# Where the sums of the first layer's weights are split, and which engine makes a low part: one change in a four-stage kernel

## Chip, core and metric

One core of a Trainium2 chip. The core has a matrix engine (TensorE, PE), VectorE (DVE), ScalarE (ACT), GpSimd (POOL) and SyncE (SP), whose queue issues nearly all DMAs. Each engine works through its own queue in order; semaphores order them against each other. The metric is the device time of one execution, in microseconds (us).

## What is computed

```python
x = attention_with_decay(q, k, v, lam)        # 2 x 768 tokens, 8 heads of 64, float32
p = domain_probs / (domain_probs.sum(-1) + 1e-9)
y = sum(p[:, e] * (relu(x @ w1[e]) @ w2[e]) for e in range(4))     # 1536 x 512, hidden 1024
h = y @ w_in                                  # hidden 2048
out = (h * sigmoid(h)) @ w_out                # 1536 x 512
```

The last two lines are the feed-forward part (FFN), which the change touches: a first layer `w_in` ("up") and a second layer `w_out` ("down").

## The kernel before

Every float32 operand of a large product is split into a high part, rounded to the matrix engine's format, and a low part, the rest; a product is the three matmul groups high x high, low x high and high x low. `split` (L144) makes the high part on ACT (L145) and the low part, a subtract, on another engine (L146), POOL unless DVE is named.

There are four stages. The first is attention, and the experts for the first 512 tokens; the second the experts for the other 1024 tokens; the third the FFN for the first 512 tokens; the fourth the FFN for the other 1024. The second and fourth use a scheme of seven products for 2 x 2 blocks, which needs sums of weight quarters. An engine's order is the order in which the program issues its instructions; nothing reorders them.

**Third stage** (the loop over `i` in `range(nb)`, 16 steps). A step does one first-layer GEMM (`gemm1`, 12 matmuls, L532, out `ph`), the sigmoid gate (`sg` on ACT, `ph` times `sg` on DVE), the split of the hidden block (`hhi` on ACT, `hlo` on DVE), and the second-layer GEMM of two steps before (`gemm2`, 12 matmuls, L589, out `po`). In steps 0 and 1 the remaining second-stage work stands in its place, and in the last two steps there is none: those GEMMs are held in `fill` for the fourth stage. Two steps, a pair, use one pair of weight blocks. `split_up` makes `ua` and `ub` (high and low) for the next pair in even steps, `split_down` `dh` and `dl` in odd ones. Beside this the stage prepares the fourth one. In even steps `left_sums` makes the four sums of the raw first-layer weights on POOL (L668) in `us`, a tile with one buffer. In odd steps `left_out` splits them (`uc` on ACT, `low` on POOL) and stores both halves to a DRAM tile `wu[i]`, and `left_kept` stores the split, unsummed blocks there. `combine` spreads eleven jobs over steps 3 to 13, which make sums (`sum`, DVE) and splits (`hi` on ACT, `lo` on DVE) of the tokens' block.

`load(0)` and `load(1)` issue the next load of raw first-layer (`u`) and second-layer (`d`) weights on SP; the buffer, one of two, must have been used up.

**Fourth stage** (the loop over `i` in `range(NV)`, 8 pairs). `pair7` issues the seven products of a pair, six matmuls each (L747, out `x`, `y`, `z`), with one or two pieces of other work from `fill` after all but the first; each is six matmuls too. `prepare` says which jobs follow which product, counted from 0. `left_in` reads the split sums of a pair and its A11 block (five slots of `ua` and `ub`), for products 1, 6, 5, 7 and 3; `left_in2` reads `uc`, for products 2 and 4. `left_in(0)` is issued in step 14 of the third stage, the others one pair ahead. `down_sums` and `down_left` make and split the sums of the second-layer weights for the second products, `down7`; `plan7` lists after which of these they are issued, and how many products or pieces later.

Of the kernel before, what the change touches and what calls it, by code (L numbers as in the profile page):

```python
# [7 lines left out]
F32 = mybir.dt.float32  # L8
F32R = mybir.dt.float32r
# [6 lines left out]
P = 128  # L16
# [10 lines left out]
HW = DM // 2  # L27
# [4 lines left out]
NV = NF  # L32


A12, A22, A21, A11 = range(4)
# [3 lines left out]
def kernel(  # L39
# [10 lines left out]
    nc = tc.nc  # L50

    def pool(stack, name, bufs=1, side="left", **kw):
        return stack.enter_context(tc.tile_pool(name=name, bufs=bufs, side=side, **kw))
# [12 lines left out]
    dram = pool(ctx, "dram", space=DRAM)  # L66

    leftp = pool(ctx, "leftp")
# [8 lines left out]

    pd = dram.tile([E, NT // GI, GI], F32, name="pd")
    wd = [dram.tile([2, P, 2 * DM], F32, name=f"wd{i}") for i in range(NV)]
    wu = [dram.tile([P, 2, 8, HW], F32, name=f"wu{i}") for i in range(NV)]  # L80

    dmask = acst.tile([P, NPAIR, 2, P], F32, name="dmask")
    qdec = acst.tile([P, NPAIR, P], F32, name="qdec")
# [30 lines left out]
    raw_t = {}  # L114
# [22 lines left out]
    def load(j, n=1):  # L137
        for _ in range(n):
            if nxt[j] < len(seq[j]):
                ph, i, src = seq[j][nxt[j]]  # L140
                nxt[j] += 1
                (load_up, load_down)[j](src, i, (ph, i))

    def split(eng, hi, lo, src):  # L144
        nc.scalar.activation(out=hi, in_=src, func=AF.Copy)  # L145
        eng.tensor_tensor(out=lo, in0=src, in1=hi.bitcast(F32), op=ALU.subtract)  # L146
# [3 lines left out]
    def up_tiles(pool_, slots=5):  # L150
        return [pool_.tile([P, slots, HW], F32R, tag=t, name=t) for t in ("ua", "ub")]

    def down_tiles(pool_):
        return [pool_.tile([P, 2, DM], F32R, tag=t, name=t) for t in ("dh", "dl")]
# [18 lines left out]
    def split_up(key, more=True):  # L173
        hi, lo = up_t[key] = up_tiles(wp)
        split(nc.gpsimd, hi[:, :4], lo[:, :4], raw_t[key, 0])
        if more:
            load(0)

    def split_down(key, eng=nc.gpsimd):
        hi, lo = down_t[key] = down_tiles(wp)  # L180
        split(eng, hi, lo, raw_t[key, 1])
        load(1)

    def up_cols(ph, f, k):
# [41 lines left out]
    def flush():  # L226
        while pending:
            pending.pop(0)()
# [9 lines left out]
    jobs = [0, 0]  # L238
# [279 lines left out]
    tmp = {}  # L518
# [137 lines left out]
    sum_t, grp_t = {}, {}  # L656

    def left_sums(key):

        u = raw_t[key, 0]  # L660
        s = leftp.tile([P, 4, HW], F32, tag="us", name="us")
        for n, (a, b, op) in enumerate([
            (u[:, A21], u[:, A22], ALU.add),
            (s[:, 0], u[:, A11], ALU.subtract),
            (u[:, A11], u[:, A21], ALU.subtract),
            (u[:, A12], s[:, 1], ALU.subtract),
        ]):
            nc.gpsimd.tensor_tensor(out=s[:, n], in0=a, in1=b, op=op)  # L668
        sum_t[key] = s
# [12 lines left out]


    def left_out(i):

        key = ("b", i)
        left_sums(key)
        src = sum_t.pop(key)

        def halves():  # L690
            load(0)
            high = leftp.tile([P, 2, 2, HW], F32R, tag="uc", name="uc").rearrange(
                "p a b n -> p (a b) n"
            )
            low = tmp["sums"].tile([P, 4, HW], F32R, tag="low", name="low")
            split(nc.gpsimd, high, low, src)
            return high, low

        def stores(tiles):
            for n, t in enumerate(tiles):  # L700
                nc.sync.dma_start(out=wu[i][:, n, 4:], in_=t.bitcast(F32))

        return halves, stores

    def left_kept(i):
        for n, t in enumerate(up_t["b", i]):
            nc.sync.dma_start(out=wu[i][:, n, :4], in_=t[:, :4].bitcast(F32))

    def left_in(i):
        grp_t[("d", i), 0] = tiles = up_tiles(wp)  # L710
        for n, t in enumerate(tiles):
            nc.sync.dma_start(out=t.bitcast(F32), in_=wu[i][:, n, A11:])

    def left_in2(i):
        t = leftp.tile([P, 2, 2, HW], F32R, tag="uc", name="uc")
# [12 lines left out]
    def unit():  # L728

        clock[0] += 1  # L730
        now = [fn for t, fn in due if t <= clock[0]]
        due[:] = [(t, fn) for t, fn in due if t > clock[0]]
        for fn in now:
            fn()

    def filler():
        if fill:
            fill.pop(0)()
        unit()
# [135 lines left out]
    def down_sums(i):  # L875

        w = raw_t[("d", i), 1].rearrange("p n (d c) -> p n d c", c=HW)
        t = tmp["d"].tile([P, 3, HW], F32, tag="ds", name="ds", bufs=2)
        for to, a, b, op in (
            (t[:, 0], w[:, 0, 1], w[:, 1, 1], ALU.add),  # L880
            (t[:, 1], t[:, 0], w[:, 0, 0], ALU.subtract),
            (t[:, 2], w[:, 1, 0], t[:, 1], ALU.subtract),
            (w[:, 0, 1], w[:, 0, 0], w[:, 0, 1], ALU.subtract),
        ):
            nc.gpsimd.tensor_tensor(out=to, in0=a, in1=b, op=op)
        d_sums[i] = {
            1: w[:, 0, 0], 2: w[:, 1, 0], 4: w[:, 1, 1],
            5: t[:, 0], 6: t[:, 1], 3: t[:, 2], 7: w[:, 0, 1],
        }

    def down_left(q):

        if q >= 7 * NV // 2:
            return
        turn = taken["dw"] % 6
        taken["dw"] += 1
        if turn < 2:
            t = tmp["d"].tile([P, 2, DM], F32R, tag="dw", name="dw", bufs=2)
        else:
            tag = ("dh", "dl")[turn % 2]  # L900
            t = wp.tile([P, 2, DM], F32R, tag=tag, name=tag)
        t = t.rearrange("p s (k c) -> p s k c", c=HW)
        for s in range(2):
            src = d_sums[q // 7 * 2 + s][ROUND[q % 7]]
            split(nc.gpsimd, t[:, s, 0], t[:, s, 1], src)
        dw_t[q] = t
# [116 lines left out]
    def plan7():  # L1023

        for g in range(NV // 2):
            q = 7 * g
            todo = [(0, 1, lambda n=q + 6: down_left(n))]
            if g + 1 < NV // 2:
                i = 2 * g + 2
                todo += [  # L1030
                    (0, 2, lambda: load(1, 2)),
                    (2, 1, lambda i=i: down_sums(i)),
                    (2, 3, lambda i=i: down_sums(i + 1)),
                ]
                for m, when, n in ((3, 1, 7), (3, 3, 8), (4, 1, 9), (4, 3, 10), (5, 2, 11), (6, 2, 12)):
                    todo.append((m, when, lambda n=q + n: down_left(n)))
            for m, when, fn in todo:
                jobs7.setdefault(q + m, []).append((when, fn))
# [118 lines left out]
    with tc.manual_schedule():  # L1157
# [62 lines left out]
        todo = {}  # L1220
# [12 lines left out]
        for i in range(NN, na):  # L1233
            gi, f = steps["a"][i]
# [89 lines left out]
        sums = ExitStack()  # L1324
        tmp["sums"] = pool(sums, "sums2", side="right")
        split_up(("b", 1), False)
        split_down(("b", 0), nc.vector)
        mixing = []
        for i in range(nb):
            flush()  # L1330
            gemm1("b", i)
            unit()
            if i < 2:
                for _ in range(KD):
                    filler()
            elif i < nb - 2:
                gemm2("b", i - 2)
            if i % 2:
                halves, stores = left
                tiles = halves()  # L1340
                for n in ([0, 1] if i == 1 else [i // 2 + 1]):
                    if n < NV:
                        left_kept(n)
                if i < nb - 1:
                    split_down(("b", (i + 1) // 2), nc.vector)
                stores(tiles)
            else:
                left = left_out(i // 2)
                if 2 <= i < nb - 2:
                    split_up(("b", i // 2 + 1), False)  # L1350
                elif i == nb - 2:
                    left_in(0)
            if i == 2:
                mixing = combine(acc_t["c", 0], acc_t["c", 1])
            elif i > 2:
                for job in mixing[i - 3:i - 2]:
                    job()
# [3 lines left out]
        tmp["d"] = pool(ctx, "dp", side="right")  # L1361
        fill += last_down("b", nb)
        plan7()
        for i in range(NV):
            jobs = {0: [lambda: left_in2(i)]}
            if i + 1 < NV:
                jobs[0].append(lambda: left_in(i + 1))
            if i == 0:
                jobs[2] = [lambda: down_sums(0)]
                jobs[4] = [lambda: down_sums(1)]  # L1370
                jobs[6] = [lambda: down_left(0), lambda: down_left(1)]
            elif i == 1:
                jobs[4] = [lambda: down_left(2), lambda: down_left(3)]
                jobs[5] = [lambda: down_left(4), lambda: down_left(5)]
            pair7(i, jobs)
        fill[-1:] = [
# [61 lines left out]
```

## Time and profile before

| | |
|---|---|
| median of 3 runs | 819.11 us (818.88 to 819.87) |
| profiled execution | 819.6 us, its span 817.8 us |
| busy: PE, DVE, ACT, POOL | 792.2, 557.3, 349.5, 504.0 us |
| PE's mean granted clock | 0.992 of full |
| third stage, from step 2 | from about 554.7 us |
| fourth stage | from about 645.6 us |

The span is what the trace covers, and the little that the execution takes beyond it lies around the program. PE's busy time is the largest of the engines'; matmuls overlap, so one that takes 389 ns follows the one before after less than that.

### The profile page before, as it was taken

To read this page: it belongs to the slowest core of one execution; us is meant where nothing else is said; L and a number is where in the kernel's file an instruction comes from. 1 tells how busy PE (TensorE), PEld (TensorE's weight loads), DVE (VectorE), ACT (ScalarE), POOL (GpSimd) and SP (SyncE) were. 2 spreads that over 40 slices of the span, in tenths; PEclk is the share of its full clock that TensorE was granted. 3 is DMA by queue.
4 is the path that set the end of the run, shared out by engine and by line. 5 is a ranking of instruction groups with operands and counts; after the bars stand their busy time and mean duration, and the time that the engine had idled before them with its cause. 6 is when DMAs were issued, how large, how long until landed. Compare 5 with 4: busy or idle time off the path is not lost.

```text
span 817.8 us, 11033 instructions
## 1 busy us (share of the span) xinstructions
PE 792.2 (97%) x4084; PEld 653.4 (80%) x4084; DVE 557.3 (68%) x785; ACT 349.5 (43%) x602; POOL 504.0 (62%) x420
## 2 busy tenths in 40 slices
PE   9999999999999999999999999999988399999997
PEld 8888888888888888888888888888766288888886
DVE  6346587786585777777777777675676256577777
ACT  4433333324454333333333333343545257745453
POOL 4846745436585666666666666657676477666753
PEclk9999999999999999999999999999999699999999
DMA  8868768453342232223222111146866726342402
GB/s 309 309 198 257 241 224 282 168 180 101 119 154 91 91 115 91 91 90 117 91 91 90 65 65 64 52 128 225 289 202 236 238 89 227 104 141 91 142 26 103
DMA packets 39479, 122.40 MB, mean 150 GB/s; under 512 B 4434, under 2 KB 4738, under 8 KB 39426
## 3 DMA queue, kind: packets, MB, share of 16 engines
q1 hardware_dynamic: 39424, 121.70, 43.9%
q8 instruction: 32, 0.52, 0.3%
q14 instruction: 21, 0.17, 0.1%
q10 hardware_dynamic: 2, 0.00, 0.0%
HBM read 93.35 MB, written 28.34 MB: 149 GB/s over the span
## 4 chain that ended last, share of the span: by engine, by line
PE 84%; DVE 4%; ACT 3%; DMA 3%; POOL 3%; issue 2%; SPq 0%; ACTq 0%; POOLq 0%; DVEq 0%
PE po L796 21%; PE ph L532 13%; PE po L589 12%; PE y L747 11%; PE z L747 8%; PE x L747 8%; PE po L976 7%; DMA wu<-low 2%; PE s L408 1%; PE xps L447 1%; DVE dl L146 1%; DMA ub<-wu 1%; POOL ub L146 1%; ACT uc L145 1%; PE xps L443 1%
## 5 line engine op out<-in xcount | busy, mean ns | idle before, releaser
L146 POOL TENSOR_TENSOR ub<-u,ua 128x1024 fp32r<-128x1024 f32 (+2 forms) x41 | 68.1, 1662 | 68.1 <-ACT ua L145 60.8
L796 PE MATMUL po<-hhi,dh 128*128 128x512 f32 x256 | 99.6, 389 | 0.0
L796 PE MATMUL po<-hhi,dl 128*128 128x512 f32 x256 | 99.6, 389 | 0.0
L796 PE MATMUL po<-hlo,dh 128*128 128x512 f32 x256 | 99.6, 389 | 0.0
L810 DVE TENSOR_TENSOR acc<-po,acc 128x512 f32<-128x512 f32 x120 | 79.4, 683 | 28.7 <-PE po L796 28.7
L146 POOL TENSOR_TENSOR dl<-d,dh 128x1024 fp32r<-128x1024 f32 (+1 forms) x33 | 77.0, 2334 | 12.3 <-ACT dh L145 12.3
L559 ACT ACTIVATE hhi<-ph 128x512 fp32r<-128x512 f32 x40 | 24.0, 599 | 126.6 <-DVE ph L553 85.3
L764 POOL TENSOR_TENSOR s<-s,s 128x512 f32<-128x512 f32 x32 | 48.6, 1520 | 31.0 <-ACT s L759 31.0
L146 POOL TENSOR_TENSOR uc<-u,uc 128x512 fp32r<-128x512 f32 x16 | 20.6, 1288 | 67.0 <-ACT uc L145 67.0
L589 PE MATMUL po<-hhi,dh 128*128 128x512 f32 (+1 forms) x208 | 57.3, 379 | 0.0
L532 PE MATMUL ph<-xhi,ub 128*128 128x512 f32 (+1 forms) x208 | 52.9, 376 | 4.5 <-POOL ub L146 4.5
L796 PEld LDWEIGHTS po<-hhi,dl 128*128 128x128 f32 x256 | 48.1, 188 | 10.1
L796 PEld LDWEIGHTS po<-hlo,dh 128*128 128x128 f32 x256 | 48.0, 188 | 9.9
L796 PEld LDWEIGHTS po<-hhi,dh 128*128 128x128 f32 x256 | 48.0, 188 | 9.9
L589 PE MATMUL po<-hhi,dl 128*128 128x512 f32 (+1 forms) x208 | 55.9, 373 | 0.0
L589 PE MATMUL po<-hlo,dh 128*128 128x512 f32 (+1 forms) x208 | 55.9, 372 | 0.0
L532 PE MATMUL ph<-xhi,ua 128*128 128x512 f32 (+1 forms) x208 | 53.8, 380 | 1.9 <-ACT ua L145 1.2
L532 PE MATMUL ph<-xlo,ua 128*128 128x512 f32 (+1 forms) x208 | 52.2, 372 | 0.0
L145 ACT ACTIVATE dh<-d 128x1024 fp32r<-128x1024 f32 (+2 forms) x56 | 47.0, 856 | 6.9 <-issue 5.5
L532 PEld LDWEIGHTS ph<-xhi,ub 128*128 128x128 f32 x208 | 37.0, 188 | 13.2 <-POOL ub L146 6.2
L560 DVE TENSOR_TENSOR hlo<-ph,hhi 128x512 fp32r<-128x512 f32 x40 | 27.7, 692 | 27.4 <-ACT hhi L559 27.4
L532 PEld LDWEIGHTS ph<-xhi,ua 128*128 128x128 f32 x208 | 36.6, 188 | 10.7 <-ACT ua L145 2.5
(215 smaller groups left out, 1989.7 us busy)
## 6 DMA issues: line engine op xcount, KB each, us to landing
u<-wts SPq DMA_DIRECT2D x32, 512.0 KB, 3.4
d<-wts SPq DMA_DIRECT2D x32, 512.0 KB, 3.3
words<-wts SPq DMA_DIRECT2D x32, 512.0 KB, 4.8
wd<-dec SPq DMA_DIRECT2D x32, 256.0 KB, 2.9
d<-wd SPq DMA_DIRECT2D x16, 512.0 KB, 4.0
qkt<-qk SPq DMA_DIRECT2D x12, 512.0 KB, 4.6
kvt<-kv SPq DMA_DIRECT2D x10, 512.0 KB, 4.3
ua<-wu SPq DMA_DIRECT2D x8, 640.0 KB, 7.9
```

The costliest lines, as they stand in the source:

```text
L145: nc.scalar.activation(out=hi, in_=src, func=AF.Copy)
L146: eng.tensor_tensor(out=lo, in0=src, in1=hi.bitcast(F32), op=ALU.subtract)
L408: nc.tensor.matmul(s[t, p // n][:, p % n], lhsT=qkt[r, 1, p], rhs=qkt[r, 0, p], start=True, stop=True,)
L532: nc.tensor.matmul(pt[:, :n], lhsT=w, rhs=x[:, k, o:o + n], start=(j == 0), stop=(j == len(ops) - 1),)
L559: nc.scalar.activation(out=hi, in_=pt, func=AF.Copy)
L560: nc.vector.tensor_tensor(out=lo, in0=pt, in1=hi.bitcast(F32), op=ALU.subtract)
L589: nc.tensor.matmul(po_t[d][:, o:o + n], lhsT=w[:, d * P:(d + 1) * P], rhs=h[:, :n], start=(begin and j == 0), stop=(last and j == 2), skip ...
L747: nc.tensor.matmul(to, lhsT=a[:, k * P:(k + 1) * P], rhs=b[:, k], start=(first and j == 0), stop=(j == len(ops) - 1), skip_group_check=not ...
L764: nc.gpsimd.tensor_tensor(out=t, in0=a, in1=b, op=ALU.add)
L796: nc.tensor.matmul(po, lhsT=w, rhs=h, start=(j == 0), stop=(j == len(ops) - 1))
L810: nc.vector.tensor_tensor(out=a, in0=po, in1=a, op=ALU.add)
L976: nc.tensor.matmul(po[:, part], lhsT=w, rhs=h[:, part], start=(j == 0 and on is None), stop=(j == len(ops) - 1), skip_group_check=on is no ...
```

## The change

The split of the sums moves from the third stage to the fourth. `left_out` stores the unsplit sums `us` (512 KB); `wu` holds three parts of four slots (high and low of the kept block, and the sums). `left_in` reads the sums into a plain tile, the A11 slot straight into `ua` and `ub`, and returns a function that splits the sums into the other four slots on ACT and POOL. For pair 0 this is called at once, in step 14; for the others the read is issued at the head of the pair before and the split follows that pair's product number 3 (`jobs[4]`). In the third stage `split_down` makes `dl` on POOL, not on DVE. In the fourth the sums and splits of the second-layer weights and their loads are issued at other places.

```diff
-    wu = [dram.tile([P, 2, 8, HW], F32, name=f"wu{i}") for i in range(NV)]
+    wu = [dram.tile([P, 3, 4, HW], F32, name=f"wu{i}") for i in range(NV)]
...
-    def split_down(key, eng=nc.gpsimd):
+    def split_down(key):
         hi, lo = down_t[key] = down_tiles(wp)
-        split(eng, hi, lo, raw_t[key, 1])
+        split(nc.gpsimd, hi, lo, raw_t[key, 1])
         load(1)
...
     def left_out(i):
-
-        key = ("b", i)
-        left_sums(key)
-        src = sum_t.pop(key)
-
-        def halves():
-            load(0)
-            high = leftp.tile([P, 2, 2, HW], F32R, tag="uc", name="uc").rearrange(
-                "p a b n -> p (a b) n"
-            )
-            low = tmp["sums"].tile([P, 4, HW], F32R, tag="low", name="low")
-            split(nc.gpsimd, high, low, src)
-            return high, low
-
-        def stores(tiles):
-            for n, t in enumerate(tiles):
-                nc.sync.dma_start(out=wu[i][:, n, 4:], in_=t.bitcast(F32))
-
-        return halves, stores
+        nc.sync.dma_start(out=wu[i][:, 2], in_=sum_t.pop(("b", i)))
...
-    def left_in(i):
+    def left_in(i, t):
+        nc.sync.dma_start(out=t, in_=wu[i][:, 2])
         grp_t[("d", i), 0] = tiles = up_tiles(wp)
-        for n, t in enumerate(tiles):
-            nc.sync.dma_start(out=t.bitcast(F32), in_=wu[i][:, n, A11:])
+        for n, to in enumerate(tiles):
+            nc.sync.dma_start(out=to[:, 0].bitcast(F32), in_=wu[i][:, n, A11])
+        hi, lo = tiles
+        return lambda: split(nc.gpsimd, hi[:, 1:], lo[:, 1:], t)
...
-            todo = [(0, 1, lambda n=q + 6: down_left(n))]
+            todo = [] if g else [(0, 1, lambda: down_left(6))]
...
-                    (0, 2, lambda: load(1, 2)),
+                    (0, 3 if g == 0 else 5, lambda: load(1, 2)),
                     (2, 1, lambda i=i: down_sums(i)),
-                    (2, 3, lambda i=i: down_sums(i + 1)),
+                    (3, 1, lambda i=i: down_sums(i + 1)),
                 ]
-                for m, when, n in ((3, 1, 7), (3, 3, 8), (4, 1, 9), (4, 3, 10), (5, 2, 11), (6, 2, 12)):
+                for m, when, n in (
+                    (4, 2, 7), (5, 2, 8), (5, 2, 9), (6, 1, 10), (6, 3, 11), (6, 5, 12), (7, 3, 13)
+                ):
...
-        split_down(("b", 0), nc.vector)
+        split_down(("b", 0))
...
             if i % 2:
-                halves, stores = left
-                tiles = halves()
+                load(0)
                 for n in ([0, 1] if i == 1 else [i // 2 + 1]):
                     if n < NV:
                         left_kept(n)
+                left_out(i // 2)
                 if i < nb - 1:
-                    split_down(("b", (i + 1) // 2), nc.vector)
-                stores(tiles)
+                    split_down(("b", (i + 1) // 2))
             else:
-                left = left_out(i // 2)
+                left_sums(("b", i // 2))
                 if 2 <= i < nb - 2:
                     split_up(("b", i // 2 + 1), False)
                 elif i == nb - 2:
-                    left_in(0)
+                    left_in(0, tmp["sums"].tile([P, 4, HW], F32, tag="low", name="low"))()
...
             if i + 1 < NV:
-                jobs[0].append(lambda: left_in(i + 1))
+                made = left_in(i + 1, leftp.tile([P, 4, HW], F32, tag="us", name="us"))
+                jobs[4] = [made]
             if i == 0:
                 jobs[2] = [lambda: down_sums(0)]
-                jobs[4] = [lambda: down_sums(1)]
+                jobs[5] = [lambda: down_sums(1)]
                 jobs[6] = [lambda: down_left(0), lambda: down_left(1)]
             elif i == 1:
-                jobs[4] = [lambda: down_left(2), lambda: down_left(3)]
+                jobs[3] = [lambda: down_left(2), lambda: down_left(3)]
                 jobs[5] = [lambda: down_left(4), lambda: down_left(5)]
```

## Rows read from the trace of the kernel before

**Rows 1.** The page, part 2: granted TensorE clock in 40 slices, tenths.

```profile
PEclk9999999999999999999999999999999699999999
```

**Rows 2.** What PE waited for: engine, line, releaser; us in total, times, longest.

```profile
PE x L747 <- DMA ua<-wu: 12.2, 1, 12.2
PE ph L532 <- POOL ub L146: 4.5, 4, 1.3
PE x L747 <- DMA ub<-wu: 1.3, 1, 1.3
```

**Rows 3.** Busy us by stretch: PE, PEld, DVE, ACT, POOL; clock, DMA share, GB/s.

```profile
554.70:633.40 78.70, 72.95 (x313) 57.83 (x311) 52.66 (x42) 37.80 (x50) 54.81 (x37) 1.00 0.68 234
...
652.00:801.40 149.40, 148.83 (x656) 122.50 (x655) 101.76 (x158) 89.14 (x188) 101.78 (x119) 1.00 0.35 116
...
599.70:612.80 13.10, 11.48 (x48) 8.86 (x48) 9.40 (x7) 5.91 (x9) 9.37 (x6) 1.00 0.71 241
```

**Rows 4.** Chain of waits, third stage: start, us, engine, tile, line.

```profile
538.53 2.72 PE ph L532 x12
...
606.50 2.58 DVE dl L146
609.08 1.68 DVE sum L634
```

**Rows 5.** Timeline of PE: start, us, operation, idle before it and what ended it.

```profile
554.69 1.07 PE L532 MATMUL ph<-xhi,ua 128*128 128x512 f32 x4
...
632.37 1.07 PE L532 MATMUL ph<-xlo,ua 128*128 128x512 f32 x4
645.63 1.19 PE L747 MATMUL x<-hi,ua 128*128 128x512 f32 x2 [12.20 <-DMA ua<-wu]
...
652.05 0.62 PE L589 MATMUL po<-hhi,dh 128*128 128x512 f32 x2
```

**Rows 6.** Timeline of DVE, POOL and ACT in the third stage.

```profile
556.09 1.47 DVE L146 TENSOR_TENSOR dl<-d,dh 128x1024 fp32r<-128x1024 f32 x1 [0.51 <-ACT dh L145]
...
560.66 2.39 POOL L146 TENSOR_TENSOR ub<-u,ua 128x1024 fp32r<-128x1024 f32 x1 [1.81 <-ACT ua L145]
...
605.60 2.40 POOL L146 TENSOR_TENSOR low<-us,uc 128x1024 fp32r<-128x1024 f32 x1 [3.35 <-ACT uc L145]
...
611.40 0.60 ACT L559 ACTIVATE hhi<-ph 128x512 fp32r<-128x512 f32 x1 [4.45 <-DVE ph L566]
...
618.74 2.41 POOL L146 TENSOR_TENSOR low<-us,uc 128x1024 fp32r<-128x1024 f32 x1 [3.35 <-ACT uc L145]
```

**Rows 7.** Busy us by stretch at the boundary, columns as in rows 3.

```profile
638.00:640.00 2.00, 0.00 (x0) 0.00 (x0) 1.30 (x2) 1.12 (x3) 0.97 (x2) 0.50 1.04 383
```

**Rows 8.** Timeline of SP's queue at the boundary: start, us to issue, transfer.

```profile
636.75 1.35 SPq L712 DMA_DIRECT2D ua<-wu  x1
```

**Rows 9.** Tile `us` from 540 to 665: ns min/median/max, first and last start.

```profile
L668 POOL TENSOR_TENSOR us<-u x16: 717/1169/1719, 542.4 to 637.6; 128x256 f32<-128x256 f32 x16
...
L145 ACT ACTIVATE uc<-us x8: 1052/1053/1056, 551.3 to 642.0; 128x1024 fp32r<-128x1024 f32 x8
```

**Rows 10.** DMA issues from 545 to 665: count, size, median us to landing.

```profile
wu<-ub SPq DMA_DIRECT2D x8, 512.0 KB, 5.6
...
d<-wd SPq DMA_DIRECT2D x7, 512.0 KB, 4.1
```

**Rows 11.** Transfers of tile `wu`, writes and reads, 540 to 665.

```profile
DMA to landing us min/median/max: 2.7/5.8/10.0
```

**Rows 12.** Timeline of PE and of ACT near the run's start.

```profile
10.72 0.78 PE L532 MATMUL ph<-xhi,ua 128*128 128x256 f32 x4 [0.67 <-ACT xhi L463]
...
10.81 0.65 ACT L145 ACTIVATE ua<-u 128x512 fp32r<-128x512 f32 x1
```

**Rows 13.** Busy us of one pair of the fourth stage, columns as in rows 3.

```profile
667.70:686.70 19.00, 19.00 (x85) 15.71 (x84) 12.50 (x20) 15.99 (x37) 15.17 (x19) 1.00 0.46 153
```

**Rows 14.** Timeline of POOL in the same pair.

```profile
678.79 1.43 POOL L146 TENSOR_TENSOR dh<-d,dh 128x256 fp32r<-128x256 f32 x2 [3.83 <-ACT dh L145]
```

More of the change, by code (lines that the diff above doesn't have):

```diff
@@ L684, in left_out @@
     def left_out(i):
-        key = ("b", i)
-        left_sums(key)
-        src = sum_t.pop(key)
-        def halves():
-            load(0)
-            high = leftp.tile([P, 2, 2, HW], F32R, tag="uc", name="uc").rearrange(
-                "p a b n -> p (a b) n"
-            )
-            low = tmp["sums"].tile([P, 4, HW], F32R, tag="low", name="low")
-            split(nc.gpsimd, high, low, src)
-            return high, low
-        def stores(tiles):
-            for n, t in enumerate(tiles):
-                nc.sync.dma_start(out=wu[i][:, n, 4:], in_=t.bitcast(F32))
-        return halves, stores
+        nc.sync.dma_start(out=wu[i][:, 2], in_=sum_t.pop(("b", i)))
     def left_kept(i):
         for n, t in enumerate(up_t["b", i]):
-            nc.sync.dma_start(out=wu[i][:, n, :4], in_=t[:, :4].bitcast(F32))
-    def left_in(i):
+            nc.sync.dma_start(out=wu[i][:, n], in_=t[:, :4].bitcast(F32))
+    def left_in(i, t):
+        nc.sync.dma_start(out=t, in_=wu[i][:, 2])
         grp_t[("d", i), 0] = tiles = up_tiles(wp)
-        for n, t in enumerate(tiles):
-            nc.sync.dma_start(out=t.bitcast(F32), in_=wu[i][:, n, A11:])
+        for n, to in enumerate(tiles):
+            nc.sync.dma_start(out=to[:, 0].bitcast(F32), in_=wu[i][:, n, A11])
+        hi, lo = tiles
+        return lambda: split(nc.gpsimd, hi[:, 1:], lo[:, 1:], t)
     def left_in2(i):
```

## The prediction

> **What bounds the kernel now.** I read the page first: the clock row shows nines except for a 6 in the 32nd of its 40 slices [rows 1]. Then the list of what TensorE (PE) waits for [rows 2]: 12.2 us once, for `ua` read back from DRAM, and four waits of the third stage for GpSimd's (POOL's) `ub`. The busy times by stage [rows 3] place them: PE has 72.95 us of work in the 78.70 of the third stage, and runs full in the fourth (148.83 of 149.40). So PE's own work sets the time nearly everywhere, and a change to the other engines counts only where PE waits or its clock is low. Two losses follow.
>
> *Third stage.* A block of 12 matmuls takes 2.72 us [rows 4]. From the start of step 2 at 554.69 [rows 5] to the end of step 15's first GEMM there are 26 blocks, 70.72 us, so unhindered it ends at 625.41. It ends at 632.37 + 1.07 = 633.44 [rows 5]: 8.03 us lost. The chain of waits names the loop: VectorE's (DVE's) `dl`, 2.58, then its `sum`, 1.68 [rows 4]. The timeline shows how: ScalarE (ACT) sits idle 4.45 us before `hhi` because DVE does `dl` and `sum` before it comes to `ph`; `ua`, and after it POOL's `ub`, follow `hhi` on ACT; POOL is idle 3.35 us for ACT's `uc` [rows 6]. A pair of steps takes 13.14 us (`low` at 605.60 and at 618.74 [rows 6]) against 4 x 2.72 = 10.88 of PE work.
>
> *Boundary.* [...] SyncE's queue (SP) issues the read of `ua` only at 636.75 [rows 8]: ahead of it stand the load of `d` that waits for DVE's last `dl`, and two stores.
>
> **The change, part by part.**
>
> *Third stage, removed:* eight ACT copies `uc` (1.05 [rows 9]), eight POOL subtracts `low` (2.40 [rows 6]) and eight 512 KB stores; eight `dl` leave DVE. *Added:* eight `dl` on POOL. There `dl` replaces `low`, both 128x1024, so I price it at 2.40 and POOL's pair stays at 9.37 us busy [rows 3]. Per pair DVE loses 2.58 and ACT 1.05; `ph` no longer stands behind `dl`, and the loop through DVE opens. What is late next?
>
> First, POOL's own order: four adds, `ub`, `dl`, where `dl` follows ACT's `dh`, whose buffer PE frees at the end of a pair. An add takes 0.72 to 1.72 [rows 9]; with at most one slow add the four take 2.9 to 3.9. After PE frees the buffer come `dh` 1.05 and `dl` 2.40, then adds and `ub` 2.39: `ub` is done 9 to 10 us after, and PE wants it 11.8 after (a pair and a third of a block). No loss from this.
>
> Second, a new wait. The buffer `us` is single; it was freed by an ACT copy and a POOL subtract, and now by the landing of its store. POOL's first add of the next pair waits for that, with `ub` and `dl` queued behind it. Loop: 0.4 to issue (behind the store of `ub`), landing, adds, `ub`. With the median landing of such a store, 5.6 [rows 10], it is 0.4 + 5.6 + 3.9 + 2.4 = 12.3 us a pair; with the shortest landing, 2.7 [rows 11], and free adds 8.4; with the longest, 10.0 [rows 11], and slow adds 19.6. The first `ub`, now done at 560.66 + 2.39 [rows 6], comes some 1 us later behind POOL's added `dl` and is wanted at 554.69 + 4 x 2.72 + 0.9 = 566.5: 2.4 of slack. Over the five turns to the last `ub`, 12.3 would lose 5 x (12.3 - 10.88) - 2.4 = 4.7 us. The queue carries 2.5 MB a pair, not 3.0, so I expect less than 5.6 and take a loss of 2.0, with 0 and 6 as near ends. Against 8.03 that gains 6.0 (2 to 8).
>
> [...]
>
> *Boundary.* `left_in(0)` still stands on SP behind the `d` load that waits for the last `dl`, but all of it comes earlier. With no third-stage loss step 13 ends at 554.69 + 24 x 2.72 = 619.97; `dh` and `dl` end at 623.4, with one hold-up such as an add meets (1.72 - 0.72) at 624.4. SP issues `d`, the sums `t` and two 128 KB reads of the first slot, 0.4 apart: `t` at 624.8. `d` lands in 4.1 [rows 10], `t`, 512 KB more, 1.3 later (at 383 GB/s [rows 7]): 629.9, and the small reads by 630.6. The first product needs only these, if waits go by slot; they do: an early GEMM starts at 10.72 while the ACT copy of the other slots of its `ua` starts at 10.81 [rows 12]. So PE idles from 625.41 to 630.6, 5.2 us. The second product needs the split: ACT until 630.95, POOL until 633.35; PE gets there at 632.4, 0.9 more. Lost: 6.1 us, whatever the third stage loses, since all moves with it. ACT and POOL stand in queue behind `t` for up to 5 us; behind them wait only step 15's `sg` and `hhi`, which PE needs after six held pieces. With the shortest landing [rows 11] the loss is 3.4, with the longest about 11. [...] Gain 15.89 - 6.1 - 1.2 = 8.6 (2.5 to 12.5).
>
> *Fourth stage, added:* seven splits (ACT 1.05, POOL 2.40: 7.4 and 16.8 us) and reads of 768 KB in place of 1280 per pair. PE is full there, and the cover is POOL's idle time: in its busiest-looking pair 15.17 busy of 19.00 [rows 13], with an idle 3.83 us ahead of the `dh` splits [rows 14]; two of these splits move one product earlier, into that hole, and the new split takes their place. On SP `t` and the small reads now stand ahead of `uc`, and `t` waits for the split of the pair before; the `d` loads come behind `uc`, not ahead. `uc` is wanted nine half blocks into a pair, 12.2 us, and even the longest landing was 10.0 [rows 11]. If the cover fails, each split shows by up to 2.40, 16.8 us in all; to gain there is at most the 0.6 that PE is idle [rows 3]. I take 0.5 lost, near the row of the hole.
>
> *Sum.* 6.0 + 8.6 - 0.5 = 14.1. The profiled execution took 819.6 (1.8 outside its span of 817.8), so 805.5; the median of the runs is 0.5 lower than that execution, hence 805.0.
>
> **Rivals.**
>
> *The fourth stage takes part of it back.* POOL lags there, its `s` for the products and its second operands come late, and PSUM banks are freed late. For: only 3.8 us are free in that pair. Against: they lie where the work moves to. At half of 16.8: 805.0 + 7.9 = 812.9. Chance 0.10.
>
> *The subtract on POOL is in the path.* `dl` and `ub` stand in one queue behind adds that DVE holds up, and POOL's 0.93 us (2.40 - 1.47) shows in each of six pairs: 5.6 us, 810.6. For: an add of 0.72 can take 1.72 [rows 9]. Against: POOL has 3.7 us a pair to spare [rows 3]. Chance 0.06.
>
> *The boundary stays.* Something holds SP or ACT longer than I place it, and `t` lands as late after PE's end as `ua` does now: only the third stage gains, 819.1 - 6.0 + 0.5 = 813.6. For: the queue order around it is unchanged. Against: the `dl` that holds it no longer waits behind DVE's other work. Chance 0.09.
>
> *Slower: the store of the sums sets the third stage.* Place: POOL's first add of a pair, waiting for `us` to land. At 16 us a pair it loses 5 x 5.12 - 2.4 = 23.2, where I count 2.0: 826.2. It makes the kernel slower from 14.9 a pair on (a loss of 17.7), a landing of 8.2 with one slow add. For: a landing of 10.0 exists [rows 11]. Against: the median is 5.6 in a fuller queue [rows 10]. Chance 0.05.
>
> **How the numbers follow.** Forecast 0.70; the rivals 0.10, 0.06, 0.09 and 0.05. The likeliest case alone spans 799 to 811. The first three rivals end inside 814, so the range is 798.5 to 814. Faster by over 0.2% (1.6 us, about what a measurement can tell from no change) 0.92; within it 0.03, from the upper ends of the first rival; slower 0.05.
>
> **What would show it.** Right: a pair of third-stage steps near 10.9 us; the first `x` matmul near 632 after a wait of about 5; POOL's `ub` no longer behind DVE; the fourth stage as long as now. Wrong: POOL idle for the store of `us` ahead of its adds; PE waiting in the fourth stage for `ub`, `uc` or the split second-layer weights. The prediction falls if PE's loss at the boundary stays above 11 us, the third stage still loses over 6, or the fourth grows by over 4.

## The result, and the profile after

The changed kernel takes 806.6 us (median of 4 runs, 805.25 to 807.17) against 819.5 for the kernel before in the same session (818.88 to 820.22): a ratio of 0.984, 95% interval 0.9823 to 0.9857. That is faster by more than the 0.2% that can be told. The forecast was 805.0, its range 798.5 to 814. The profiled execution took 806.6 us, its span is 804.8 (817.8 before), the mean granted clock 0.995. A few line numbers shift: L747 is now L732, L712 is L692 and L695, L717 is L702, L927 is L912, L922 is L907, L976 is L961.

The clock row of the page still has one slice that isn't a 9, and it is an 8 where a 6 stood [rows 1]:

```profile
PEclk9999999999999999999999999999999899999999
```

What PE waited for from the third stage into the fourth (engine, line, releaser; us in total, times, longest), which answers to [rows 2]:

```profile
PE x L732 <- DMA ua<-wu: 3.2, 1, 3.2
PE ph L532 <- POOL ub L146: 1.0, 2, 0.6
PE y L732 <- POOL ub L146: 0.7, 1, 0.7
PE po L961 <- ACT ohi L905: 0.5, 1, 0.5
```

The wait of 12.2 is down to 3.2 and the third stage's 4.5 to 1.0; the last line is new and lies in the fourth stage. The timeline of PE gives the losses by the prediction's own measure (start, us, operation, idle before it), as [rows 5] did:

```profile
555.10 1.07 PE L532 MATMUL ph<-xhi,ua 128*128 128x512 f32 x4
...
626.50 1.07 PE L532 MATMUL ph<-xlo,ua 128*128 128x512 f32 x4
630.76 0.70 PE L732 MATMUL x<-hi,ua 128*128 128x512 f32 x2 [3.19 <-DMA ua<-wu]
...
633.94 1.22 PE L732 MATMUL y<-hi,ub 128*128 128x512 f32 x2 [0.67 <-POOL ub L146]
...
635.81 1.05 PE L589 MATMUL po<-hhi,dh 128*128 128x512 f32 x2
```

Third stage: 626.50 + 1.07 - 555.10 = 72.47 for the same 70.72 of blocks, 1.75 lost (8.03 before). Boundary, up to the first `po`: 635.81 - 627.57 - 2.72 = 5.52 lost (15.89 before). There the clock falls, as the stretches show (PE, PEld, DVE, ACT, POOL busy; clock, DMA share, GB/s; compare [rows 7]):

```profile
628.00:632.00 4.00, 1.24 (x6) 1.05 (x7) 0.14 (x2) 1.55 (x2) 2.29 (x4) 1.00 0.91 345
632.00:634.00 2.00, 1.33 (x5) 0.56 (x3) 1.34 (x2) 0.68 (x2) 1.88 (x1) 0.55 0.36 39
...
638.00:640.00 2.00, 2.00 (x8) 1.65 (x7) 0.00 (x0) 0.00 (x0) 0.05 (x1) 0.74 0.05 12
640.00:642.00 2.00, 2.00 (x10) 1.65 (x10) 0.00 (x0) 0.60 (x1) 1.08 (x1) 1.00 0.00 0
```

In this execution 1.52 us more are lost in the rest of pair 0 because of that. The table gives, for the profiled run of every kernel below, the same two losses (0 would be no loss), the first three pairs of the fourth stage, and the rest, all read from PE's timeline. "Pair 0" is from the first `po` to pair 1's first `x`, "pair 1" and "pair 2" from `x` to `x`, "pairs 3 on" from pair 3's `x` to the end of PE's last matmul; the last column is all of it, from the start of step 2.

| profiled run | 3rd stage lost | wait for `ua` | boundary lost | pair 0 | pair 1 | pair 2 | pairs 3 on | from step 2 |
|---|---|---|---|---|---|---|---|---|
| before | 8.03 | 12.20 | 15.89 | 15.64 | 15.64 | 19.07 | 111.58 | 259.28 |
| after | 1.75 | 3.19 | 5.52 | 17.16 | 17.13 | 19.31 | 111.33 | 245.64 |
| a_dl_dve | 0.64 | 4.40 | 6.92 | 15.67 | 17.13 | 19.31 | 111.35 | 244.47 |
| b_dl_pool | 6.42 | 11.21 | 14.97 | 15.72 | 15.64 | 19.08 | 111.56 | 256.83 |
| c_us_two | 0.16 | 4.38 | 6.63 | 15.67 | 17.15 | 19.30 | 111.32 | 243.69 |
| d_early | 2.94 | none | -0.16 | 15.66 | 17.12 | 19.31 | 111.33 | 239.64 |
| h_before_early | 9.64 | none | -0.16 | 24.99 | 15.64 | 19.06 | 111.61 | 254.22 |
| f_oldplan | 1.67 | 3.25 | 5.24 | 15.67 | 16.32 | 23.66 | 113.98 | 249.98 |
| e_pair1 | 3.38 | 3.59 | 5.12 | 15.65 | 16.29 | 20.16 | 111.35 | 245.39 |
| g_cde | 0.16 | none | 1.00 | 16.52 | 15.64 | 19.75 | 111.37 | 237.87 |
| j_load | 2.63 | 3.07 | 5.16 | 15.66 | 16.31 | 19.94 | 115.56 | 248.70 |
| i_best | 0.16 | none | -0.16 | 15.85 | 17.24 | 19.91 | 111.35 | 237.80 |
| k_best | 0.16 | none | -0.16 | 15.86 | 19.03 | 19.23 | 111.35 | 238.91 |

After against before: 6.28 gained in the third stage, 10.37 at the boundary, 1.52 and 1.49 lost in pairs 0 and 1. With 0.41 of a later start of step 2 and 0.2 behind PE's last matmul that is the 13.0 by which the span is shorter. The four runs with the changed third stage as it is (after, f, e, j) lose 1.67 to 3.38 there, so a difference below 2 us in one such profile proves nothing by itself; the runs with two buffers for the sums (c, g, i, k) lose 0.16 each. Step 2 itself starts anywhere from 554.38 to 556.19 us in these profiles, and that lies in the times of whole runs too: two kernels that are close are better compared by the last column.

### The profile page after: what moved, and what is told of

Its sections match the earlier page's. It is cut to its first block, busy times and chain, and to the rows that moved or that the text cites. A ratio compares the mean times of both kernels' runs of the same rounds, so it can differ in the third digit from the quotient of the medians.

```text
span 804.8 us, 11035 instructions
## 1 busy us (share of the span) xinstructions
PE 792.6 (98%) x4084; PEld 654.4 (81%) x4084; DVE 544.9 (68%) x777; ACT 350.3 (44%) x602; POOL 510.1 (63%) x428
## 4 chain that ended last, share of the span: by engine, by line
PE 87%; POOL 5%; DMA 2%; ACT 2%; DVE 1%; issue 1%; SPq 0%; POOLq 0%; ACTq 0%
PE po L781 22%; PE ph L532 13%; PE po L589 13%; PE y L732 12%; PE po L961 9%; PE z L732 8%; PE x L732 7%; POOL ub L146 2%; DMA wu<-us 2%; PE s L408 2%; PE xps L447 1%; POOL us L668 1%; PE xps L443 1%; DMA low<-wu 1%; POOL dl L146 0%
## 5 line engine op out<-in xcount | busy, mean ns | idle before, releaser
L146 POOL TENSOR_TENSOR dl<-d,dh 128x1024 fp32r<-128x1024 f32 (+1 forms) x41 | 96.8, 2363 | 29.8 <-ACT dh L145 29.8
L146 POOL TENSOR_TENSOR ub<-us,ua 128x1024 fp32r<-128x1024 f32 x23 | 56.0, 2434 | 17.4 <-ACT ua L145 17.4
L749 POOL TENSOR_TENSOR s<-s,s 128x512 f32<-128x512 f32 x32 | 44.2, 1383 | 35.4 <-ACT s L744 35.4
```

The costliest lines, as they stand in the source:

```text
L749: nc.gpsimd.tensor_tensor(out=t, in0=a, in1=b, op=ALU.add)
```

## The experiments

**What opens the third stage.** Theory: `dl` left VectorE. Two runs do one half each. a_dl_dve is the changed kernel with `dl` back on VectorE:

```diff
...
-        split_down(("b", 0))
+        split_down(("b", 0), nc.vector)
...
-                    split_down(("b", (i + 1) // 2))
+                    split_down(("b", (i + 1) // 2), nc.vector)
```

> The changed kernel with one part undone: the third stage's eight `dl` subtracts go back to VectorE; the sums stay unsplit there. Theory (VectorE's queue was the third stage's bound, and taking `dl` off it opens the loop): the loop is the old one less ACT's `uc` of 0.95 us, 12.2 us a pair against 10.9 of TensorE work, so the third stage loses 2 to 5 us more than in the changed kernel, and the read for pair 0 comes that much later after TensorE's end: 809 to 813. Rival (what counts is that copies, subtracts and stores left the stage, whichever engine makes `dl`): 806.6, as the changed kernel. Second rival (`dl` on GpSimd costs 0.93 us each on the path, and undoing it gains): 801 to 805.

Measured: 804.63 us (801.97 to 806.31), ratio 0.9817 (0.9793 to 0.9841): the theory's 809 to 813 missed, and the four runs spread over both rivals. b_dl_pool is the kernel before with the opposite edit, `dl` on GpSimd and nothing else.

> The kernel before with that one part done alone: `dl` on GpSimd in the third stage, the sums still split and stored there. GpSimd then has four adds, `ub`, `low` and `dl` in a pair: 7.8 + 2.4 = 10.2 us without hold-ups, 11.8 with those of the trace of before, against 10.9 of TensorE work. Theory (VectorE was the bound of the third stage, the queue order that of the boundary): the third stage gains some 4 us of its 8, the boundary keeps most of its wait because the read still stands behind two more stores: 812 to 816. Rival (GpSimd becomes the bound, so the two parts only work together): 819 or more.

Measured: 818.28 us (816.68 to 819.17), ratio 0.9983 (0.9973 to 0.9992), outside both expectations; the third stage still loses 6.42. So the theory fell both ways: `dl` need not leave VectorE, and its leaving alone is worth 1.2 us by the medians. What opens the stage is that the split of the sums (`uc`, `low`) and one of its two stores are gone; which of these it takes, no run separates. Groups of DVE instructions in the third stage (busy us, mean ns | idle before them) show one way in which it can work. Before:

```profile
L146 DVE TENSOR_TENSOR dl<-d,dh 128x1024 fp32r<-128x1024 f32 x7 | 17.0, 2423 | 7.7 <-ACT dh L145 7.7
...
L634 DVE TENSOR_TENSOR sum<-acc,sum 128x1024 f32<-128x1024 f32 x2 | 3.5, 1756 | 0.0
```

In a_dl_dve:

```profile
L146 DVE TENSOR_TENSOR dl<-d,dh 128x1024 fp32r<-128x1024 f32 x7 | 8.6, 1226 | 6.1 <-ACT dh L145 5.8 <-DMA wu<-ub 0.3
...
L634 DVE TENSOR_TENSOR sum<-acc,sum 128x1024 f32<-128x1024 f32 x2 | 2.4, 1218 | 0.0
```

The same seven `dl` take 1.23 us in place of 2.42, half. Before, `low` runs on POOL from 605.60 to 608.00 [rows 6] and DVE's `dl` from 606.50 to 609.08 [rows 4]: it starts within POOL's subtract and ends 1.08 after it. So do all six `dl` of that stage that start within a `low`: each takes 2.57 to 2.59 and ends 1.08 to 1.09 after POOL's. In a_dl_dve POOL idles there, waiting for a store, and PE hardly waits:

```profile
POOL us L668 <- DMA wu<-us: 42.2, 7, 10.5
PE ph L532 <- POOL ub L146: 0.2, 1, 0.2
```

That POOL's operations stretched VectorE's two-input ones is what these times suggest; no run here varies it alone. The durations are 1.23 us without POOL at work, and 2.58 when `dl` started 1.5 us ahead of POOL's end.

**The new wait, for the store of the sums.** c_us_two gives the third stage's sums two buffers:

```diff
-        s = leftp.tile([P, 4, HW], F32, tag="us", name="us")
+        tag = "uc" if key[0] == "b" and key[1] % 2 else "us"
+        s = leftp.tile([P, 4, HW], F32, tag=tag, name="us")
```

> The changed kernel with two buffers for the unsplit sums in the third stage (odd pairs use the idle `uc` buffer), so GpSimd's adds no longer wait for the store of the pair before (8.1 us in four waits in the changed kernel's trace). Theory (these waits are almost wholly covered; TensorE itself waits 1.0 us for `ub`): 805 to 806.6, third stage better by 0.5 to 1.5. Rival (the store sets the stage's pace): 803 or less.

Measured: 804.26 us (803.84 to 806.42), ratio 0.9821 (0.9806 to 0.9836), between the theory and its rival. The third stage's loss falls to 0.16, as in every later run with this edit, so the wait for the store was what was left of it. But the wait for `ua` grows from 3.19 to 4.38: the reads start no earlier, and PE only reaches them sooner. The time is within the uncertainty of the changed kernel's. POOL's waits in the changed kernel are

```profile
POOL dl L146 <- ACT dh L145: 17.4, 5, 8.3
POOL us L668 <- DMA wu<-us: 8.1, 4, 3.1
```

and those for the store are gone from the list of c_us_two, where only ACT holds POOL:

```profile
POOL dl L146 <- ACT dh L145: 24.3, 7, 8.3
POOL ub L146 <- ACT ua L145: 2.0, 1, 2.0
```

**The boundary.** d_early reads pair 0's sums in step 11 and its A11 slots at the head of step 13, and splits at that step's end:

```diff
             if i % 2:
+                if i == nb - 5:
+                    ahead = tmp["sums"].tile([P, 4, HW], F32, tag="low", name="low")
+                    nc.sync.dma_start(out=ahead, in_=wu[0][:, 2])
                 load(0)
+                if i == nb - 3:
+                    grp_t[("d", 0), 0] = first_up = up_tiles(wp)
+                    for n, to in enumerate(first_up):
+                        nc.sync.dma_start(out=to[:, 0].bitcast(F32), in_=wu[0][:, n, A11])
...
+                if i == nb - 3:
+                    split(nc.gpsimd, first_up[0][:, 1:], first_up[1][:, 1:], ahead)
...
-                elif i == nb - 2:
-                    left_in(0, tmp["sums"].tile([P, 4, HW], F32, tag="low", name="low"))()
```

> The changed kernel with pair 0's sums read in step 11, its A11 slots at the head of step 13, and the split at that step's end, all ahead of the `d` load that waits for the last `dl`. Theory (what is left of the boundary, a wait of 3.2 us, one of 0.7 and a clock at its lower level from about 632 to 639.5, comes from the place of these reads in SyncE's queue): no wait for `ua` over 1 us, the clock stays at the full level, 5 to 7 us gained: 799.5 to 801.5. Rival 1 (ACT or GpSimd are the late ones there, not the queue): 804 to 806. Rival 2 (the clock falls there whatever the wait is): the wait goes, the lower level stays, 802.5 to 804.

Measured: 800.7 us (800.03 to 801.04), ratio 0.9771 (0.9756 to 0.9786), as the theory had it. There is no wait left at the boundary, PE is busy throughout, and the granted clock stays at 1.00:

```profile
625.00:635.00 10.00, 10.00 (x46) 8.24 (x45) 4.76 (x5) 4.43 (x8) 8.67 (x7) 1.00 0.55 209
```

Was it then only the place in SP's queue? h_before_early is the kernel before with its own `left_in(0)` moved from step 14 to the head of step 13.

> The kernel before, with the reads of pair 0's left slots (both halves, as before) issued one step earlier, at the head of step 13 instead of step 14; nothing else changed, the split still in the third stage. Theory: the 12.2 us wait at the boundary is only the place of these reads in SP's queue, behind the stores that wait for the last splits; read a step earlier they have landed, the wait and the low clock go, and the third stage keeps its own loss of 8.0: boundary loss 15.9 -> 0 to 2, time 804 to 807. Rival: the amount of data decides (both halves go through memory, twice as much as sums), so that some 5 us of wait and the low clock stay: 809 to 812.

Measured: 815.41 us (815.32 to 815.55), ratio 0.9947 (0.9932 to 0.9962), and both expectations missed. The wait for `ua` did go, with all 15.9 us of the boundary's loss; but pair 0 takes 24.99 in place of 15.64, and the third stage loses 1.6 more, in a profile where the granted clock is 0.50 from 630 to 633. ACT's waits just behind the boundary name the reason for pair 0, and PE's timeline the price:

```profile
ACT s L1051 <- DMA wu<-low: 5.9, 1, 5.9
```

```profile
650.06 1.22 PE L747 MATMUL y<-hi,ua 128*128 128x512 f32 x2 [7.05 <-ACT s L1051]
```

The last pair's split sums are stored at 645.52 on SP, and ACT's `s`, the fourth stage's first copy, waits for that store; the trace names the store, and that `s` takes over the memory of `low` is inferred. The clock stands at 0.50 from 647 to 653 beside that. In the kernel before, ACT waits for the same store, until 650.8, but PE, held at `ua` until 645.6, comes to this product only later:

```profile
ACT s L1051 <- DMA wu<-low: 7.7, 1, 7.7
```

So an earlier read alone uncovers the next wait. The change takes away the late split and its store, and with them gone the earlier read of d_early pays off.

**The fourth stage.** f_oldplan is the changed kernel with all jobs of the fourth stage back in the gaps of before (the diff's `plan7` lines and `jobs[5]`, `jobs[3]` undone, the split of the sums kept at gap 4).

> The kernel after, with every job of the fourth stage (the sums and left sides of the seventh products, the load) back in the gap where the kernel before has it; the split of the next pair's sums stays at gap 4, ahead of them. Theory: GpSimd has room in the fourth stage for the split wherever it stands, so the moved jobs carry little: pair 0 to pair 2 takes 32 to 35 us (34.3 after, 31.3 before), the rest 130.6 to 132, time 805 to 809. Rival (the fourth stage takes part back unless the jobs are spread): the second half of the stage loses 3 us or more: 810 to 815.

Measured: 810.55 us (809.65 to 811.5), ratio 0.9889 (0.9873 to 0.9906): the rival was right. Pair 2 takes 23.66, and the pairs behind it 2.6 more than in the changed kernel. From pair 1 on it is 6.2 us more; the medians are only 3.95 apart, as pair 0 takes 1.49 less here, with a shorter low clock. What SP waited for around pair 2:

```profile
SPq L123 <- POOL dw L146: 12.4, 2, 12.1
```

The load of the second layer's next weights waits 12.1 us for a buffer that POOL frees, and the next pair's reads stand behind it; PE then waits 1.8 us for `uc`, until 682.2, and the granted clock is 0.74 between 680 and 685. j_load leaves that load where the change has it:

```diff
-                    (0, 2, lambda: load(1, 2)),
+                    (0, 3 if g == 0 else 5, lambda: load(1, 2)),
```

> The kernel after with the fourth stage's jobs back in the gaps of before, as in the run that took 810.55 us, but the load of the second layer's next weights left where the kernel after has it, behind the next pair's reads in SP's queue. Theory: the 4.4 us that pair 2 lost there (23.66 us against 19.31) come from that one load, whose wait for a buffer that GpSimd frees (12.1 us) holds the next pair's reads; with the load behind the reads pair 2 takes 19.3 to 20.2 us and the time is 805 to 808. Rival: GpSimd's own load (the sums and left sides are ready late) made the loss, the place of the load does not matter: pair 2 stays above 22 us, 809.5 to 811.5.

Measured: 809.88 us (808.61 to 811.32), ratio 0.9882 (0.9863 to 0.9901). Pair 2 is back at 19.94, as the theory said; but the pairs from 3 on take 115.56 in place of 111.33, so the time does not move beyond its uncertainty and the theory's 805 to 808 missed. The load's place in SP's queue decides pair 2; behind it sums and operands are ready late. PE's waits there, from 688 on, are short, and the clock stays at 1.00:

```profile
PE po L961 <- ACT po L944: 1.6, 2, 1.1
PE y L732 <- DVE olo L907: 0.9, 3, 0.3
```

They make 2.5 of the 4.2 us. The weight loads, which run ahead of PE (in the changed kernel one starts at 663.29 for a matmul at 663.52), wait for more in the same stretch, 6.3 us in all against 1.2 in the changed kernel: for the same two, and `z` for DVE's work on `y` (1.5). How much of that PE feels stays open. e_pair1 tries the other end, the 1.49 us that pair 1 pays for the new places:

```diff
-                jobs[3] = [lambda: down_left(2), lambda: down_left(3)]
+                jobs[4] = [lambda: down_left(2), lambda: down_left(3), made]
```

> The kernel after, with pair 1's first two left sides put back from gap 3 to gap 4, ahead of the split. Theory: the 1.5 us that pair 1 takes longer than before (17.13 against 15.64) come from their four ScalarE copies, which stand ahead of the rounding of the first output's left side; with the copies a gap later pair 1 takes 15.6 to 16.1 us, time 805.0 to 805.7. Rival: the late end of pair 0's sums alone (GpSimd's split ahead of them) makes the output late, the copies do not: pair 1 stays at 17 or more, 806.3 to 807.

Measured: 804.8 us (804.14 to 805.82), ratio 0.9819 (0.9804 to 0.9834), both figures of the theory narrowly missed. Pair 1 falls to 16.29, so the ACT copies were in its way, but pair 2 rises to 20.16: together 36.45, against 36.44 in the changed kernel. Nothing was won by it, though the median is 1.8 us lower: from step 2 the two profiles are 0.25 apart, with 1.63 more lost in the third stage and 1.51 less in pair 0, which this edit doesn't touch.

**Together.** g_cde is c, d and e in one.

> The kernel after with three edits together: two buffers for the sums in the third stage, pair 0's sums read and split a step or two earlier, and pair 1's first left sides a gap later. Theory (the three terms add, each where its own run or trace shows it): 800.7 with the early read alone, less 1.6 to 2.3 for the wait on the store, less 1.0 to 1.5 for pair 1: 797 to 799.5. Rival: the early split takes GpSimd in the step where the second buffer gave the time, the third stage keeps 2 to 3 us of loss: 799.5 to 801.

Measured: 799.42 us (798.22 to 799.85), ratio 0.975 (0.9735 to 0.9764), at the theory's upper edge. Now PE comes to pair 0 before its split is done (0.9 us for `ub`) and later waits 0.4 for `uc`. i_best, which keeps the three edits, puts that split ahead of `split_down` in step 13, swaps the two buffers of the sums, and reads pair 0's `uc` ahead of pair 1's sums:

```diff
-        tag = "uc" if key[0] == "b" and key[1] % 2 else "us"
+        tag = "uc" if key[0] == "b" and key[1] % 2 == 0 else "us"
...
+                if i == nb - 3:
+                    split(nc.gpsimd, first_up[0][:, 1:], first_up[1][:, 1:], ahead)
                 if i < nb - 1:
                     split_down(("b", (i + 1) // 2))
-                if i == nb - 3:
-                    split(nc.gpsimd, first_up[0][:, 1:], first_up[1][:, 1:], ahead)
...
-            jobs = {0: [lambda: left_in2(i)]}
+            jobs = {}
+            if i:
+                jobs[0] = [lambda: left_in2(i)]
+            else:
+                left_in2(0)
```

> The version with three edits that took 799.42 us, with the early split put ahead of the second layer's split in its step, the buffers of the third stage's sums taken the other way round, and the reads of pair 0's second group ahead of those of pair 1. Theory: the two waits left at the boundary (0.9 us for GpSimd's split of pair 0, 0.4 for the read of the second group) go, the rest stays: 797.6 to 798.8. Rival: the second layer's split is then late by 2.4 us in a stretch where GpSimd has no room, and the third stage loses 1 to 3 us: 799.5 to 801.5.

Measured: 798.26 us (797.83 to 798.98), ratio 0.9741 (0.9726 to 0.9755), the lowest median here, and well below the changed kernel's; from g_cde it can't be told, as the intervals overlap. From step 2 the profiles of the two take 237.80 and 237.87: boundary and pair 0 gain 1.8 us over g_cde, and pair 1 gives 1.6 of it back. The third stage and the boundary run without a gap; the wait for `uc` that should go is now pair 1's. What PE waits for between 554 and 700 is

```profile
PE x L733 <- DMA uc<-wu: 0.8, 1, 0.8
PE y L733 <- DVE olo L908: 0.6, 1, 0.6
```

k_best moves, beside that, pair 1's split to gap 3 and pair 0's second sums back to gap 4:

```diff
             if i == 0:
+                jobs[3] = jobs.pop(4)
                 jobs[2] = [lambda: down_sums(0)]
-                jobs[5] = [lambda: down_sums(1)]
+                jobs[4] = [lambda: down_sums(1)]
```

> As the run beside it, with pair 1's split moved from gap 4 to gap 3 of pair 0, and pair 0's second sums back from gap 5 to gap 4. Theory: the second layer's sums end a gap earlier, and pairs 1 and 2 together take 34.7 to 35.2 us as before the change instead of 35.4 to 36.4: 0.3 to 1.2 us below the run beside it, 797 to 798.2. Rival: pair 1's sums have not landed by gap 3, GpSimd waits for them with the other work behind it: equal or up to 1.5 us above.

Measured: 799.58 us (799.34 to 800.82), ratio 0.9759 (0.9745 to 0.9774): 1.3 above i_best, no run of one within the range of the other, and 1.1 more from step 2. The rival had the size, and the sums that have not landed; but the engine that waits for them is ACT, 2.63 us before its half of the split (0.60 in i_best), with the copies for `ohi` behind it. POOL starts its half no earlier than in i_best, and PE then waits for `olo`; pair 1 grows to 19.03:

```profile
639.43 1.06 ACT L145 ACTIVATE ua<-us 128x1024 fp32r<-128x1024 f32 x1 [2.63 <-DMA us<-wu]
...
647.69 0.73 PE L733 MATMUL y<-hi,ua 128*128 128x512 f32 x2 [1.61 <-DVE olo L908]
```

## Why the prediction was right, and where its steps were not

The time came out 1.6 us above the forecast and well inside its range. By its three terms (6.0 + 8.6 - 0.5 against the profile's 6.3 + 8.9 - 1.5, with pair 0's 1.5 counted to the boundary; 0.6 more went at the ends) it was right in size, but not in every reason, and in part by luck.

*Third stage, size right, reason wrong.* Forecast loss 2.0, measured 1.75. The step "`ph` no longer stands behind `dl`, and the loop through DVE opens" failed: with `dl` still on VectorE the loss is no greater (0.64), and with `dl` alone moved it stays at 6.42. I had priced VectorE's operations at their durations of before; `dl` takes half once POOL's `low` is gone, 1.23 us in a_dl_dve against 2.42. The `dl` of 1.47 [rows 6], which the rival of the subtract on POOL sets against 2.40, was no undisturbed one, since POOL's adds ran from 555.74 to 558.15 beside its 556.09 to 557.56:

```profile
556.43 1.72 POOL L668 TENSOR_TENSOR us<-u 128x256 f32<-128x256 f32 x1
```

The wait for the store was placed rightly. I worked out 12.3 us a pair for its loop, and the chain of waits has 12.06 for one of them, from one store to the next (start, us, what):

```profile
599.20 5.26 DMA wu<-us
...
611.26 5.00 DMA wu<-us
...
620.34 2.35 POOL ub L146
622.68 2.36 POOL dl L146
...
625.43 4.85 DMA low<-wu
...
631.50 2.39 POOL ub L146
```

Other pairs take 10.97 to 12.68. From the store at 564.55 to that at 623.08 five turns take 11.71 each, and my sum with that, 5 x (11.71 - 10.88) - 2.4, gives the 1.75 that was lost. The longest landing of the sums was 6.1 us, so the slower rival, which needed 8.2, did not come. The landing of 10.0 that spoke for it [rows 11] was a 640 KB read; the longest store there took 8.2.

*Boundary, sum right, parts off.* By this chain `dl` ends at 625.04 and the sums land at 630.28; I had 624.4 and 629.9. PE's end was late by more (627.57, not 625.41), so it waited 3.2 where I had 5.2. The clause "whatever the third stage loses, since all moves with it" failed: where PE ends earlier the wait can grow, as after and c_us_two show (1.75 + 3.19 and 0.16 + 4.38). Waits of 3.9 in all stand against the 6.1 of the forecast. The other way the clock was under-priced. The forecast's 15.89 is the loss measured in the kernel before; its two waits, 12.20 and 1.33 [rows 2], leave 2.36 of it, beside a clock of 0.50 [rows 7]. No run shows the forecast's 1.2 for the clock, my estimate at half of that 2.36; in its place the changed kernel lost 5.52 - 3.19 - 0.67 + 1.52 = 3.2, more than the 2.4 of the longer wait. That the two errors cancel is luck. The 3.2 is also of this execution: in f, e and j, with the same code at the boundary, the waits are 3.4 to 3.6, the low clock is shorter and costs 1.5 to 1.8, and pair 0 takes 15.65 to 15.67.

*Fourth stage, mis-sized.* I took 0.5, the row of POOL's idle hole [rows 14]; it is 1.5, in pair 1. There `down_sums(1)` stands behind the 2.40 of the new split, what follows on POOL is a good microsecond later, and four ACT copies moved to gap 3 stand ahead of a first operand. 1.1 of it stand here on PE's timeline, as the wait and slower matmuls behind it:

```profile
664.93 0.74 PE L961 MATMUL po<-ohi,dw 128*128 128x512 f32 x2 [0.55 <-ACT ohi L905]
```

Some 0.3 more lie ahead of it, where the weight loads wait 0.6 us for `uc`, a wait that I had put at nothing. That POOL had room "where the work moves to" held only because the jobs were spread over more gaps: with them at their old places (f, and j but for one load) the time is 3.3 to 4.0 us longer. Against the kernel before, f takes 7.7 us more from pair 1 on, nearly the 8.4 that this rival counted. Given 0.10, it was closer than I thought.

*The other rivals.* `dl` on POOL was not in the path: a_dl_dve, without that move, is not separable from the changed kernel (0.9817, 0.9793 to 0.9841, against 0.984, 0.9823 to 0.9857). The operation itself is slower on POOL, 2.40 us against 1.23 on VectorE while POOL idles, and the kernel's time shows no difference. That the boundary stays is refuted for the whole change, but b_dl_pool and h_before_early show how near it lay: `dl` off VectorE alone leaves a wait of 11.2 us, and an earlier read alone moves 9.35 us into pair 0.

## What to carry to other kernels

Price a shared loop's operations by what runs beside them after the change, not by their durations before: here VectorE's `dl` went from 2.42 to 1.23 us with POOL's `low` gone. Where two stages meet, ask what the next wait is if the first goes (another store, a buffer, the same read), since an earlier read alone may only uncover it; and count a short wait in front of PE at more than its length if the granted clock falls with it: here waits of 3.19 and 0.67 us stood beside another 3.2 us lost while the clock was at 0.50.

## What was not expected of the hardware

After a wait of 3.2 us the granted clock went from 1.00 to 0.50, as it had within the wait of 12.2. It fell at 632.2, when PE had been at work again for 1.5 us and ahead of the wait of 0.7, and was back at 639.0. Behind shorter waits it fell too, but not always: to a mean of 0.74 from 680 to 685 behind 1.8 us in f_oldplan, while the clock stayed at 1.00 behind 1.6 in k_best and 0.9 in g_cde. In h_before_early it stood at 0.50 in the third stage, where PE had just waited 0.41 and 1.25, and the same two waits in the kernel before left it at 1.00:

```profile
630.00:633.00 3.00, 3.00 (x8) 2.32 (x8) 1.83 (x3) 1.83 (x3) 0.21 (x1) 0.50 1.00 406
```

So the length of the last wait alone does not tell what the clock does. In d_early and i_best, without these waits, it stays at 1.00.

VectorE's 128x1024 operation with two inputs takes 1.22 to 1.23 us in a_dl_dve where POOL idles, against 1.47 for the `dl` of before beside POOL's adds [rows 6], and 2.58 for one beside POOL's `low` [rows 4]. POOL's own operations stretch as well: its 128x256 add takes 0.72 to 1.72 before and 0.72 to 1.78 after. In the third stage of before, each add of 1.59 to 1.72 starts while VectorE runs a 128x1024 operation, and none of the shorter ones (0.72 to 0.75) does.
